# The first product of ten of the dense layer's sixteen weight groups by Strassen's scheme: seven products of sums of quarters in place of eight

## The chip, the cores and the metric

The kernel runs on one core of a Trainium2 chip. The metric is device time in microseconds for one execution, the median over runs. The core has five engines with a queue of instructions each: TensorE (PE in the profile, with PEld for its loads of weights), VectorE (DVE), ScalarE (ACT), GpSimd (POOL) and SyncE (SP), which issues most DMAs here.

## What is computed

Attention over a window of 32 keys and sums of 32-key blocks, then a dense layer of four experts, each weighted by its probability for each token, then a layer with eight experts of which each token takes one at most. The change is in the dense layer. Its reference, with N = 1536 tokens, D = 512, four experts and F = 1024 features:

```python
def _moe_ref(x, domain_probs, w1, w2):
    p = domain_probs / (domain_probs.sum(-1, keepdims=True) + 1e-09)
    out = np.zeros((N, D), dtype=np.float32)
    for e in range(E):
        h = np.maximum(x @ w1[e], 0.0)
        out += p[:, e:e + 1] * (h @ w2[e])
    return out
```

## The kernel before

Features are taken in 16 groups of 256, four to an expert. A group has two pieces of 128 features (`cc`), and x is cut into four chunks of 128 rows (`c`). Products are made in parts, so as to come near to float32: of each operand there is a high part (rounded, names with `h`) and a low part (the rest, names with `l`), and each product is three matmuls, high by high, low by high and high by low, into one bank of PSUM.

- **First product** (`part_a`, L357): for a block of 512 tokens and a piece of 128 features, 4 chunks x 3 matmuls of 512 columns into bank 0 or 1. The weights stand in the array, the tokens stream. ScalarE takes the relu out of the bank (L364, `hh`), VectorE the low part (L365, `hl`).
- **Second product** (`part_b`, L377): for each tile of 128 tokens 3 matmuls a piece, 6 a group, into banks 2 to 5. VectorE multiplies by the probability and adds to the result `acc` (L387).
- **Weights**: `load_w` issues two DMAs a group on SP into `raw`, 512 KB each; `split_w` rounds a half of them on ScalarE (L96) and subtracts on VectorE (L97). The parts of two groups stand side by side (`g % 2`), the raw weights of one.

Groups 0 and 1 run together with the attention, in blocks of two tiles (256 columns). Groups 2 to 13 go by themselves, three blocks of 512 tokens each; groups 14 and 15 run together, with the routing of the last layer between their blocks. The order of work up to group 13 is a scheduler's, which takes the program in the order of emission and moves instructions within each engine by its own costs; from group 14 on (`manual_schedule`) it is the order of emission. Each engine does its queue in order. The loop over `chunks` emits the first product of a piece and the second product of the piece before, and then a split of the next group's weights. `route_setup` (tables and memsets on GpSimd, two loads on SP) and 12 stores of zeros to `out` are emitted when the attention has ended.

Of the kernel before, what the change touches and what calls it, by code (L numbers as in the profile page):

```python
# [9 lines left out]
F32 = mybir.dt.float32  # L10
# [14 lines left out]
def attention_moe_kernel(  # L25
# [46 lines left out]
    wtiles = {}  # L72

    def load_w(g):
        wh = wps[g % 2].tile([P, 2 * KC * GF], F32R, name=f"wh{g}", tag="wh")
        wl = wps[g % 2].tile([P, 2 * KC * GF], F32R, name=f"wl{g}", tag="wl")
# [13 lines left out]
        wtiles[g] = (raw, wh, wl)  # L90

    def split_w(g, i):
        raw, wh, wl = wtiles[g]
        w = KC * GF // 2
        s, r = slice(i * w, (i + 1) * w), raw[i // 2][:, i % 2 * w : (i % 2 + 1) * w]
# [41 lines left out]
    # a band: the columns from 20 - 4 * i on average the rows of the i-th 128 tokens over 32  # L137
# [72 lines left out]
    def k_win(b, t):  # L210
        """Keys that the queries of a unit see, their sums behind them."""
# [15 lines left out]
    def fold_rows(dst, t):  # L227
        """Sums the eight rows of each partition on GpSimd."""
# [9 lines left out]
    def v_acc(b, i):  # L238
        """Sums over groups of tokens on TensorE."""
# [96 lines left out]
    chunks = []  # L336

    def moe_block(gs, t0, nt):
        """Work of a block of tokens with the weights of groups gs, one chunk of 128 features at a time."""
# [7 lines left out]
        def part_a(ci, c):  # L347
            g, cc = gs[ci // ncc], ci % ncc
            _, wh, wl = wtiles[g]
# [21 lines left out]
        def part_b(ci, t):  # L371
            g, cc = gs[ci // ncc], ci % ncc
            _, wh, wl = wtiles[g]
            hh, hl = hs[ci]
            f0 = KC * GF + cc * DM
# [26 lines left out]
    # parts of the base slots: (place of the expert in the order, its first rank)  # L402
# [11 lines left out]
    # slots: halves of the first product in parts, whether the second product is, engines of the low parts  # L414
# [4 lines left out]
    # slots whose parts are made from a slot on  # L419
# [52 lines left out]
    def route_block(t0, k):  # L472
        """Work that routes k tiles of tokens, in order; None where the next piece waits for VectorE."""
# [132 lines left out]
    def decode(name, c):  # L606
        """Rows and gates from sums of codes; a place that no token has gives a row behind the last."""
# [9 lines left out]
    def count_all(col):  # L617
        """Number of tokens listed so far for each expert, the same in each partition."""
# [4 lines left out]
    def early_pick():  # L623
        """Orders the experts by their tokens so far; the last two get more room."""
# [9 lines left out]
        # place in the lists of each place of the base slots  # L634
# [24 lines left out]
    def early_close():  # L659
        """Later tokens of the picked expert come behind the places of the early slot."""  # L660
# [9 lines left out]
    def list_sel(name, off, nt, done=None):  # L670
        """Marks, for 128 consecutive places of the lists, the tokens of the first nt tiles that stand there."""
# [76 lines left out]
    def load_units(limit=None):  # L748
        """Loads in order into the tiles that no emitted or coming reader needs."""
# [16 lines left out]
    def more_units(a, b):  # L766
        """Pairs of tiles of rows that have gone out."""
# [17 lines left out]
    def split_next():  # L785
        """High and low parts of the next half unit, into the place of one that the products have left."""
# [13 lines left out]
    def want_split(es, one, two, low):  # L800
        """Parts wanted by a slot: of the last halves of the first product, of the second; low: engines of the low parts."""
# [19 lines left out]
    def slot_trans(name, xg, b):  # L821
        """Rows of a slot the other way round: as they are, and in parts."""
# [4 lines left out]
        if one < 2:  # L827
            # the early slot's stand where rows have gone out
# [112 lines left out]
    # TensorE's clock rises only after some time of work  # L941
# [24 lines left out]
    def a_list():  # L966
        """Attention work in order of emission: (TensorE cost, function, unit completed)."""
# [108 lines left out]
    for g in range(2, last - 1):  # L1076
        for i in range(3):
            moe_block((g,), 4 * i, 4)
# [9 lines left out]
    rstack = ExitStack()  # L1088
# [12 lines left out]
    def expert(s):  # L1101
        """Register with the expert at place s of the order of the slots."""
# [20 lines left out]
    for ch in chunks:  # L1123
# [13 lines left out]
        if ch["gs"] == (last - 1,) and first and ch["t0"] == 0:  # L1137
            ctx.enter_context(tc.manual_schedule())
        micros = list(ch["a"])
# [18 lines left out]
        if p1:  # L1158
            if ch["last"] and blk == len(PH1) - 1:
                run_to(len(alist))  # L1160
                astack.close()
                rpool = rstack.enter_context(tc.tile_pool(name="route", bufs=1, side="right", reuse_waits="tile"))
# [8 lines left out]
                load_w(2)  # L1171
                for i in range(4):
                    split_w(2, i)
        elif not fin:
# [146 lines left out]
```

## Time and profile before

| | us |
|---|---|
| runs (three) | 714.49, 716.11, 717.57 |
| median | 716.11 |
| span of the profiled execution | 717.6 |
| TensorE busy | 696.9 |
| VectorE busy | 358.9 |
| ScalarE busy | 199.2 |
| GpSimd busy | 68.1 |

The span runs from the first to the last instruction of one execution. [...] Idle time is put down to the engine and the tile that was waited for. GpSimd's work lies in the attention and in the last layer; in the middle of the span it has none. Durations of single instructions hold for an engine alone; where operations of one kind follow each other their ends overlap a little with the next start, and a row of n gives the better price.

### The profile page before, as it was taken

To read this page: it belongs to the slowest core of one execution; us is meant where nothing else is said; L and a number is where in the kernel's file an instruction comes from. 1 tells how busy PE (TensorE), PEld (TensorE's weight loads), DVE (VectorE), ACT (ScalarE), POOL (GpSimd) and SP (SyncE) were. 2 spreads that over 40 slices of the span, in tenths; PEclk is the share of its full clock that TensorE was granted. 3 is DMA by queue.
4 is the path that set the end of the run, shared out by engine and by line. 5 is a ranking of instruction groups with operands and counts; after the bars stand their busy time and mean duration, and the time that the engine had idled before them with its cause. 6 is when DMAs were issued, how large, how long until landed. Compare 5 with 4: busy or idle time off the path is not lost. (4 is left out here: it accounts for less than half of the span.)

```text
span 717.6 us, 10481 instructions
## 1 busy us (share of the span) xinstructions
PE 696.9 (97%) x3951; PEld 553.9 (77%) x3951; DVE 358.9 (50%) x919; ACT 199.2 (28%) x505; POOL 68.1 (9%) x142
## 2 busy tenths in 40 slices
PE   6889999999999999999999999999999999799996
PEld 6779888888888888888888888888888888574361
DVE  5788655354353444353443544452525565585441
ACT  4556564221120212021221202021211223171340
POOL 5216400000000000000000000000000003331230
PEclk9999999999999999999999999999999999899999
DMA  9987211520101101010101101010100187467991
GB/s 233 234 208 168 63 46 24 207 87 0 59 14 46 59 0 59 1 58 1 59 0 59 37 22 59 0 59 1 58 1 0 60 311 268 142 247 281 412 409 53
DMA packets 39876, 73.77 MB, mean 103 GB/s; under 512 B 16740, under 2 KB 19812, under 8 KB 39824
## 3 DMA queue, kind: packets, MB, share of 16 engines
q1 hardware_dynamic: 38592, 70.31, 30.3%
q0 software_dynamic: 960, 2.25, 0.9%
q8 instruction: 32, 0.52, 0.3%
q10 hardware_dynamic: 272, 0.52, 0.2%
q14 instruction: 20, 0.16, 0.1%
HBM read 66.10 MB, written 7.86 MB: 103 GB/s over the span
## 5 line engine op out<-in xcount | busy, mean ns | idle before, releaser
L387 DVE SCALAR_TENSOR_TENSOR acc<-bank,pr,acc 128x512 f32<-128x512 f32 x163 | 113.3, 744 | 112.3 <-PE bank L377 112.3
L357 PE MATMUL bank<-xh,wh 128*128 128x512 f32 (+2 forms) x448 | 161.8, 363 | 0.0
L357 PE MATMUL bank<-xl,wh 128*128 128x512 f32 (+2 forms) x448 | 161.1, 360 | 0.0
L357 PE MATMUL bank<-xh,wl 128*128 128x512 f32 (+2 forms) x448 | 160.7, 359 | 0.0
L364 ACT ACTIVATE hh<-bank 128x512 fp32r<-128x512 f32 (+2 forms) x112 | 60.0, 536 | 345.6 <-PE bank L357 345.6
L377 PE MATMUL bank<-wh,hh 128*128 128x512 f32 x384 | 152.2, 396 | 0.0
L377 PE MATMUL bank<-wh,hl 128*128 128x512 f32 x384 | 146.8, 393 | 3.9 <-DVE hl L365 3.9
L377 PE MATMUL bank<-wl,hh 128*128 128x512 f32 x384 | 150.1, 391 | 0.0
L365 DVE SCALAR_TENSOR_TENSOR hl<-bank,hh 128x512 fp32r<-128x512 f32 (+2 forms) x112 | 68.3, 610 | 144.9 <-ACT hh L364 144.9
L357 PEld LDWEIGHTS bank<-xh,wh 128*128 128x128 f32 x448 | 84.1, 188 | 13.4 <-issue 0.4
L357 PEld LDWEIGHTS bank<-xl,wh 128*128 128x128 f32 x448 | 84.4, 188 | 12.8 <-DVE xl L333 0.2
L357 PEld LDWEIGHTS bank<-xh,wl 128*128 128x128 f32 x448 | 84.4, 188 | 11.9
L377 PEld LDWEIGHTS bank<-wh,hl 128*128 128x128 f32 x384 | 71.9, 188 | 19.6 <-DVE hl L365 4.8
L377 PEld LDWEIGHTS bank<-wh,hh 128*128 128x128 f32 x384 | 72.4, 188 | 16.2 <-issue 2.3
L377 PEld LDWEIGHTS bank<-wl,hh 128*128 128x128 f32 x384 | 72.4, 189 | 13.6 <-issue 0.2
L810 POOL DMA_INDIRECT xg<-out_dram,ixx x1 | 1.2, 1236 | 474.5 <-DVE acc L387 474.5
L289 ACT ACTIVATE sm<-sm,mn 128x120 f32<-128x120 f32 x96 | 36.7, 385 | 19.0 <-DVE mn L284 18.8
L96 ACT CAST wh<-raw 128x512 fp32r<-128x512 f32 x57 | 31.3, 618 | 30.4 <-PE bank L377 27.2
L97 DVE TENSOR_TENSOR wl<-raw,wh 128x512 fp32r<-128x512 f32 x60 | 37.7, 685 | 3.3 <-ACT wh L96 3.3
L273 PE MATMUL bank<-kw,qbd 128*128 128x120 f32 x192 | 27.3, 292 | 4.1 <-DMA qbd<-in_q_dram 3.7
L273 PEld LDWEIGHTS bank<-kw,qbd 128*128 128x128 f32 x192 | 24.7, 203 | 5.3 <-ACT kw L223 3.9
L284 DVE CUSTOM_DVE_ANT_0 sm<-bank,masks 128x120 f32<-128x120 f32 x96 | 21.3, 276 | 9.7 <-PE bank L273 9.6
(236 smaller groups left out, 629.7 us busy)
## 6 DMA issues: line engine op xcount, KB each, us to landing
raw<-in_moe_w_dram SPq DMA_DIRECT2D x30, 512.0 KB, 3.9
ra<-in_moe_w_dram SPq DMA_DIRECT2D x27, 512.0 KB, 9.1
rb<-in_moe_w_dram SPq DMA_DIRECT2D x21, 512.0 KB, 6.9
acc<-in_moe_w_dram SPq DMA_DIRECT2D x15, 512.0 KB, 9.3
vwin<-in_v_dram SPq DMA_DIRECT2D x24, 192.0 KB, 4.6
kt<-in_k_dram SPq DMA_DIRECT2D x8, 384.0 KB, 6.0
qbd<-in_q_dram SPq DMA_DIRECT2D x24, 128.0 KB, 5.6
out_dram<-xg SPq DMA_DIRECT2D x12, 256.0 KB, 2.9
```

Of the source, the lines that this page charges most:

```text
L96: (nc.gpsimd.tensor_copy if (g, i) in WPOOL else nc.scalar.copy)(wh[:, s], r)
L97: nc.vector.tensor_sub(wl[:, s], r, wh[:, s].bitcast(F32))
L273: nc.tensor.matmul(ps[:, h * WC : (h + 1) * WC], qb[b, t // 2][:, t % 2, h, :], kwin[b, t // 4][:, t % 4, h, :], start=True, stop=True,)
L284: nc.vector.tensor_tensor_reduce(out=sm[:, h, :], in0=ps[:, h * WC : (h + 1) * WC], in1=masks[:, m, :], scale=-0.125, scalar=3.0e38, op0=A ...
L289: nc.scalar.activation(sm[:, h, :], sm[:, h, :], AF.Exp, bias=mn[:, h : h + 1], scale=-1.0, accum_out=su[:, h : h + 1],)
L357: nc.tensor.matmul(b[:, :n], wt[:, f0 : f0 + P], xt[:, c, :], start=(c == 0 and i == 0), stop=(c == KC - 1 and i == 2),)
L364: nc.scalar.activation(hh[:, :n], b[:, :n], AF.Relu)
L365: nc.vector.scalar_tensor_tensor(out=hl[:, :n], in0=b[:, :n], scalar=0.0, in1=hh[:, :n].bitcast(F32), op0=ALU.max, op1=ALU.subtract,)
L377: nc.tensor.matmul(bank[2 + t], ht[:, t * P : (t + 1) * P], wt[:, f0 : f0 + DM], start=(ci == 0 and i == 0), stop=(ci == nch - 1 and i == 2),)
L387: nc.vector.scalar_tensor_tensor(out=a, in0=bank[2 + t], scalar=sc, in1=a, op0=ALU.mult, op1=ALU.add,)
L810: nc.gpsimd.indirect_dma_start(out=xg, out_offset=None, in_=out[:rows, :], in_offset=bass.IndirectOffsetOnAxis(ap=ix, axis=0), bounds_chec ...
```

## The change

For groups 4 to 13 (`SGROUPS`) the first product is no longer made block by block. The tokens are taken as two pairs of equal parts: `l`, tokens 512 to 1023 and 1024 to 1535 (512 columns a matmul), and `s`, tokens 0 to 255 and 256 to 511 (256 columns). x for a pair is cut into four quarters, two halves of the rows (256 each) by the two parts of the tokens, and the group's weights into four quarters, the two halves of the rows by the two pieces of features. In place of the eight products of quarters there are seven, of quarters and sums of quarters, each of 2 chunks x 3 matmuls (`burst`): p1, p5, p6, p3, p7, p2, p4 in that order. The sums between products are made in three ways: by summing on in a bank (p6 and p7 into the bank that holds a copy of p1; p3 into p5's; p2 into p1's; p4 into the bank of p1 + p6 + p7), by copies to SBUF on ScalarE (`s5`, `u2`) and by adds on VectorE (`u2` = p3's bank + `u2`; `s5` = p7's bank + `s5`).

- **Sums of x** (`x_sums`), once for all ten groups: 36 operations of 512 columns on VectorE (12 of them make x from its parts, 12 are sums, 12 low parts) and 12 roundings on ScalarE. They are emitted with groups 2 and 3, three steps after each chunk.
- **Sums of weights** (`w_steps`), each group: four operations on GpSimd, one of which overwrites a quarter of the raw weights, then rounded on ScalarE and subtracted on VectorE in two pieces.
- **Order** (`middle`): written out by hand from group 4 on. After each of the 14 products of a group stands one tile of the second product (six matmuls, the two pieces one behind the other), save after the third and the sixth product of the short pair; the steps for the next group's weights are dealt out by the table `at`. Tiles left over go on with the next group, the last seven with group 14. Tiles use banks 2 to 4 in turn.
- **Set-up of the routing**, its loads and the 12 stores of zeros: at the first piece of group 14. `load_w(15)` is ahead of them on SP. What the parts of weights are kept in is divided (`w_parts`), so that those of the second product are taken later.
- One matmul into bank 7 is added ahead of group 4.

```diff
+    SGROUPS = range(4, E1 * NG - 2)
+    PAIRS = {"l": (4 * P, 4 * P), "s": (0, 2 * P)}
...
+            def whole(i, j):
+                h, l = x_quarter(p, i, j, c)
+                nc.vector.tensor_add(xt[f"{i + 1}{j + 1}"], h.bitcast(F32), l.bitcast(F32))
+            def total(i, a, b):
+                nc.vector.tensor_sub(ts[i], a, b)
+                nc.scalar.copy(xsum[p][0][:, i, c, :], ts[i])
+            def low(i):
+                nc.vector.tensor_sub(xsum[p][1][:, i, c, :], ts[i], xsum[p][0][:, i, c, :].bitcast(F32))
...
+    def w_steps(g):
...
+            t = scr["w"].tile([P, 3, 2, P], F32, name=f"ws{g}", tag="ws")
+            tt = nc.gpsimd.tensor_tensor
+            tt(out=t[:, 1], in0=a11, in1=a21, op=ALU.subtract)
+            tt(out=a21, in0=a21, in1=a22, op=ALU.add)
+            tt(out=t[:, 0], in0=a21, in1=a11, op=ALU.subtract)
+            tt(out=t[:, 2], in0=a12, in1=t[:, 0], op=ALU.subtract)
...
+        def sum_parts(i):
+            (h, l), t = wtiles[g][3:]
+            s = slice(0, 2) if i == 0 else slice(2, 3)
+            nc.scalar.copy(h[:, s], t[:, s])
+            nc.vector.tensor_sub(l[:, s], t[:, s], h[:, s].bitcast(F32))
...
+            lambda: load_w(g), sums if mid else no, lambda: split_w(g, 1), lambda: split_w(g, 0),
+            (lambda: sum_parts(0)) if mid else no, (lambda: sum_parts(1)) if mid else no,
+            lambda: split_w(g, 2), lambda: split_w(g, 3),
...
+        ba, be, bb = bank[state_["i"] % 2], bank[6], bank[7 - 2 * (state_["i"] % 2)]
...
+        def burst(b, w, x, start):
+            for c in range(2):
+                for i, (a, m) in enumerate(((0, 0), (0, 1), (1, 0))):
+                    nc.tensor.matmul(
+                        b[:, :n], w[c][a], x[c][m], start=start and c == 0 and i == 0, stop=c == 1 and i == 2,
...
+        def p1():
+            burst(ba, wq(0, 0), xq(0, 0), True)
+            nc.scalar.copy(bb[:, :n], ba[:, :n])
+        def p5():
+            burst(be, wq(1, 0), xs(0), True)
+            nc.scalar.copy(tmp("s5"), be[:, :n])
+        def p6():
+            burst(bb, wsum(0), xs(1), False)
+            nc.scalar.copy(tmp("u2"), bb[:, :n])
+        def p3():
+            burst(be, wsum(2), xq(1, 1), False)
+            nc.vector.tensor_add(fs["u2"], be[:, :n], fs["u2"])
+            part(0, 1, fs["u2"])
+        def p7():
+            burst(bb, wsum(1), xs(2), False)
+            nc.vector.tensor_add(fs["s5"], bb[:, :n], fs["s5"])
+            part(1, 1, fs["s5"])
+        def p2():
+            burst(ba, wq(0, 1), xq(1, 0), False)
+            part(0, 0, ba[:, :n])
+        def p4():
+            burst(bb, wq(1, 1), xs(3), False)
+            part(1, 0, bb[:, :n])
...
+        nc.tensor.matmul(bank[7], wh[:, :P], wh[:, :512], start=True, stop=True)
+        at = {0: (0,), 2: (1,), 4: (2,), 5: (3,), 7: (4,), 8: (5,), 9: (6,), 11: (7,)}
+        for g in SGROUPS:
+            nxt = w_steps(g + 1)
+            i = 0
+            for p in "ls":
+                bursts, tiles = pair_work(g, p, state_)
+                for b in bursts:
+                    b()
+                    for k_ in at.get(i, ()):
+                        nxt[k_]()
+                    if i not in (9, 12) and todo:
+                        todo.pop(0)()
+                    i += 1
+                todo += tiles
```

`part` takes the relu (ScalarE) and its low part (VectorE) as before, from a bank or from `u2` and `s5`.

Three places show what the engines' queues hold now. In the names, `hl5_4_1` is the low part of the relu of group 5, block of tiles from 4 on, piece 1; `hls01_s5_01` the same of group 5's short pair; `w2l6` is the low part of group 6's second weights, `wsl6` that of its sums; `u2s5` and `s5s5` are the short pair's sums of group 5.

VectorE in the middle, group 5, before: splits, then low parts and updates of the result.

```order
L97 TENSOR_TENSOR wl6_2445<-raw6_0_2446,wh6_2444 128x512 x2
L97 TENSOR_TENSOR wl6_2445<-raw6_1_2447,wh6_2444 128x512 x2
L365 SCALAR_TENSOR_TENSOR hl5_0_1_2463<-bank1_62,hh5_0_1_2462 128x512
L365 SCALAR_TENSOR_TENSOR hl5_4_0_2493<-bank0_61,hh5_4_0_2492 128x512
L387 SCALAR_TENSOR_TENSOR acc_74<-bank2_63,pr_75,acc_74 128x512
L387 SCALAR_TENSOR_TENSOR acc_74<-bank3_64,pr_75,acc_74 128x512
L387 SCALAR_TENSOR_TENSOR acc_74<-bank4_65,pr_75,acc_74 128x512
L387 SCALAR_TENSOR_TENSOR acc_74<-bank5_66,pr_75,acc_74 128x512
L365 SCALAR_TENSOR_TENSOR hl5_4_1_2527<-bank1_62,hh5_4_1_2526 128x512
```

VectorE in the middle now, short pair of group 5, from the last sum of weights on:

```order
L474 TENSOR_TENSOR wsl6_2497<-ws6_2491,wsh6_2496 128x256
L570 SCALAR_TENSOR_TENSOR acc_74<-bank3_64,pr_75,acc_74 128x512
L102 TENSOR_TENSOR w2l6_2621<-raw6_1_2458,w2h6_2620 128x512
L544 TENSOR_TENSOR u2s5_2618<-bank6_67,u2s5_2618 128x256
L525 SCALAR_TENSOR_TENSOR hls01_s5_01_2632<-u2s5_2618,hhs01_s5_01_2631 128x256
L570 SCALAR_TENSOR_TENSOR acc_74<-bank4_65,pr_75,acc_74 128x512
L549 TENSOR_TENSOR s5s5_2601<-bank5_66,s5s5_2601 128x256
L525 SCALAR_TENSOR_TENSOR hls11_s5_11_2650<-s5s5_2601,hhs11_s5_11_2649 128x256
```

Between the updates of `acc` there are now adds out of banks 6 and 5, and the split of the next group's second weights stands right ahead of them.

VectorE at the end of groups 0 and 1, before (block of tiles from 10 on, then group 2):

```order
L365 SCALAR_TENSOR_TENSOR hl0_10_0_1656<-bank0_61,hh0_10_0_1655 128x256
L365 SCALAR_TENSOR_TENSOR hl0_10_1_1680<-bank1_62,hh0_10_1_1679 128x256
L365 SCALAR_TENSOR_TENSOR hl1_10_0_1702<-bank0_61,hh1_10_0_1701 128x256
L97 TENSOR_TENSOR wl2_1825<-raw2_0_1826,wh2_1824 128x512 x2
L97 TENSOR_TENSOR wl2_1825<-raw2_1_1827,wh2_1824 128x512 x2
L365 SCALAR_TENSOR_TENSOR hl1_10_1_1724<-bank1_62,hh1_10_1_1723 128x256
L365 SCALAR_TENSOR_TENSOR hl2_0_0_1851<-bank0_61,hh2_0_0_1850 128x512
```

The same place now, from the fourth operation behind `hl0_10_0` on; three more of the same kinds stand ahead of these rows:

```order
L431 TENSOR_TENSOR t1l0_1801<-x22l0_1799,t0l0_1800 128x512
L428 TENSOR_TENSOR x11l1_1950<-xh1_79,xl1_80 128x512
L102 TENSOR_TENSOR w1l2_1751<-raw2_0_1752,w1h2_1750 128x512
L370 SCALAR_TENSOR_TENSOR hl0_10_1_1684<-bank1_62,hh0_10_1_1683 128x256
L428 TENSOR_TENSOR x12l1_1951<-xh1_79,xl1_80 128x512
L435 TENSOR_TENSOR xsll_1744<-t0l0_1800,xslh_1743 128x512
L435 TENSOR_TENSOR xsll_1744<-t2l0_1802,xslh_1743 128x512
L431 TENSOR_TENSOR t3l0_1803<-x21l0_1798,t1l0_1801 128x512
L428 TENSOR_TENSOR x22l1_1953<-xh1_79,xl1_80 128x512
L435 TENSOR_TENSOR xsll_1744<-t1l0_1801,xslh_1743 128x512
L370 SCALAR_TENSOR_TENSOR hl1_10_0_1706<-bank0_61,hh1_10_0_1705 128x256
```

Sums of x (L428 makes x from its parts, L431 a sum, L435 a low part) and the first splits of group 2 stand between the low parts of the relus.

GpSimd behind the attention's last copies, before:

```order
L266 COPY vwin2_168<-vsm1_912 24x512
L266 COPY vwin3_169<-vsm1_912 24x512
L430 IOTA io_1739 128x128
L433 IOTA cf_1742 128x12
L434 IOTA cf_1742 128x12
L438 MEMSET tri_1747 128x128
```

GpSimd in the middle now (40 rows of this kind, four for each of groups 4 to 13, stand between those copies and the tables):

```order
L463 TENSOR_TENSOR ws6_2491<-raw6_0_2457 128x256
L464 TENSOR_TENSOR raw6_0_2457<-raw6_0_2457 128x2x128
L465 TENSOR_TENSOR ws6_2491<-raw6_0_2457 128x256
L466 TENSOR_TENSOR ws6_2491<-raw6_0_2457,ws6_2491 128x256
L463 TENSOR_TENSOR ws7_2732<-raw7_0_2698 128x256
```

The tables (`io`, `cf` and on) have moved behind them, to group 14.

## Rows read from the trace of the kernel before

**Rows 1.** The page's first part: busy time, share of the span, instructions

```profile
PE 696.9 (97%) x3951; PEld 553.9 (77%) x3951; DVE 358.9 (50%) x919; ACT 199.2 (28%) x505; POOL 68.1 (9%) x142
```

**Rows 2.** Busy times by stretch; one group of weights in the middle

```profile
core 0: us, PE busy (x) PEld busy (x) DVE busy (x) ACT busy (x) POOL busy (x), PEclk, DMA share, GB/s
182.60:215.30 32.70, 32.70 (x146) 27.08 (x145) 14.36 (x22) 5.78 (x10) 0.00 (x0) 1.00 0.11 34
```

**Rows 3.** The waits: who for whom, us in total, times, longest

```profile
ACT hh L364 <- PE bank L357: 345.6, 95, 4.8
```

**Rows 4.** Timeline of ScalarE: start, duration, line, operation, idle time before it

```profile
153.79 0.60 ACT L364 ACTIVATE hh<-bank 128x512 fp32r<-128x512 f32 x1 [4.84 <-PE bank L357]
159.23 0.60 ACT L364 ACTIVATE hh<-bank 128x512 fp32r<-128x512 f32 x1 [4.84 <-PE bank L357]
```

**Rows 5.** Timeline, all engines: a product's last matmul and its reader

```profile
300.25 0.39 PE L357 MATMUL bank<-xh,wl 128*128 128x512 f32 x1
300.67 0.60 ACT L364 ACTIVATE hh<-bank 128x512 fp32r<-128x512 f32 x1 [4.84 <-PE bank L357]
```

**Rows 6.** Timeline of TensorE: matmuls of 256 columns back to back

```profile
131.93 0.28 PE L357 MATMUL bank<-xh,wh 128*128 128x256 f32 x1
...
134.33 0.40 PE L377 MATMUL bank<-wh,hh 128*128 128x512 f32 x1
```

**Rows 7.** Groups by line and shape: weight loads (busy, mean ns)

```profile
L357 PEld LDWEIGHTS bank<-xh,wl 128*128 128x128 f32 x448 | 84.4, 188 | 11.9
```

**Rows 8.** The same view: operations on VectorE, ScalarE and GpSimd

```profile
L387 DVE SCALAR_TENSOR_TENSOR acc<-bank,pr,acc 128x512 f32<-128x512 f32 x163 | 113.3, 744 | 112.3 <-PE bank L377 112.3
L365 DVE SCALAR_TENSOR_TENSOR hl<-bank,hh 128x256 fp32r<-128x256 f32 x28 | 11.7, 416 | 17.4 <-ACT hh L364 17.3
L364 ACT ACTIVATE hh<-bank 128x256 fp32r<-128x256 f32 x28 | 10.6, 379 | 17.5 <-PE bank L357 17.4
L97 DVE TENSOR_TENSOR wl<-raw,wh 128x512 fp32r<-128x512 f32 x60 | 37.7, 685 | 3.3 <-ACT wh L96 3.3
L96 ACT CAST wh<-raw 128x512 fp32r<-128x512 f32 x57 | 31.3, 618 | 30.4 <-PE bank L377 27.2 <-DMA raw<-in_moe_w_dram 3.1
L230 POOL TENSOR_TENSOR acc<-acc 96x256 f32<-96x256 f32 x4 | 3.4, 842 | 0.0
L798 POOL TENSOR_TENSOR sl<-ra,sh 128x512 fp32r<-128x512 f32 x7 | 8.9, 1283 | 14.5 <-ACT sh L797 14.5
```

**Rows 9.** Timeline, end of the first two groups: VectorE, then TensorE

```profile
133.68 0.42 DVE L365 SCALAR_TENSOR_TENSOR hl<-bank,hh 128x256 fp32r<-128x256 f32 x1 [0.79 <-ACT hh L364]
139.38 2.50 DVE L97 TENSOR_TENSOR wl<-raw,wh 128x512 fp32r<-128x512 f32 x4 [1.20 <-ACT wh L96]
140.90 0.62 PE L377 MATMUL bank<-wh,hl 128*128 128x512 f32 x2
```

**Rows 10.** Timeline: VectorE and GpSimd at the same time, two places

```profile
71.39 0.74 POOL L230 TENSOR_TENSOR acc<-acc 96x256 f32<-96x256 f32 x1
71.48 0.42 DVE L365 SCALAR_TENSOR_TENSOR hl<-bank,hh 128x256 fp32r<-128x256 f32 x1
669.22 3.43 DVE L798 TENSOR_TENSOR sl<-acc,sh 128x512 fp32r<-128x512 f32 x1
669.57 1.29 POOL L798 TENSOR_TENSOR sl<-acc,sh 128x512 fp32r<-128x512 f32 x1
670.83 1.26 POOL L798 TENSOR_TENSOR sl<-ra,sh 128x512 fp32r<-128x512 f32 x1
```

**Rows 11.** Set-up of the routing: issues, a relu; loads (count, KB, us to landing)

```profile
125.20 7.26 SPq L1168 DMA_DIRECT2D out_dram<-xg  x12
534.59 0.60 ACT L364 ACTIVATE hh<-bank 128x512 fp32r<-128x512 f32 x1 [4.84 <-PE bank L357]
559.69 0.40 SPq L486 DMA_DIRECT2D out_dram<-acc  x1
raw<-in_moe_w_dram SPq DMA_DIRECT2D x30, 512.0 KB, 3.9
```

More of the change, by code (lines that the diff above doesn't have):

```diff
@@ L72, in attention_moe_kernel, with w_parts @@
     wtiles = {}
+    def w_parts(g, i):
+        return [wps[g % 2].tile([P, KC * GF], F32R, name=f"w{i}{n}{g}", tag=f"w{i}{n}") for n in "hl"]
     def load_w(g):
-        wh = wps[g % 2].tile([P, 2 * KC * GF], F32R, name=f"wh{g}", tag="wh")
-        wl = wps[g % 2].tile([P, 2 * KC * GF], F32R, name=f"wl{g}", tag="wl")
+        w1t = w_parts(g, 1)
         if g == 0:
@@ L348, in part_a @@
             g, cc = gs[ci // ncc], ci % ncc
-            _, wh, wl = wtiles[g]
+            wh, wl = wtiles[g][1]
             if c == 0:
@@ new lines, in middle @@
+    def middle(todo):
+        todo = list(todo)
+        state_ = dict(i=0, b=0)
+        wh = wtiles[SGROUPS[0]][1][0]
+        nc.tensor.matmul(bank[7], wh[:, :P], wh[:, :512], start=True, stop=True)
[13 more added lines that the diff above has]
+                todo += tiles
+        return todo
@@ L1075, in attention_moe_kernel @@
         moe_block(gs, t0, n)
-    for g in range(2, last - 1):
+    for g in range(2, SGROUPS[0]):
         for i in range(3):
@@ L1138, in attention_moe_kernel @@
             ctx.enter_context(tc.manual_schedule())
+            prev = dict(gs=(last - 2,), last=True, b=middle(prev["b"]))
+            load_w(last)
         micros = list(ch["a"])
@@ L1161, in attention_moe_kernel @@
                 astack.close()
+                scr["w"] = sstack.enter_context(tc.tile_pool(name="msum", bufs=1, side="right", reuse_waits="tile"))
+                for p_, (_, n_) in PAIRS.items():
+                    xsum[p_] = [scr["w"].tile([P, 4, 2, n_], F32R, name=f"xs{p_}{q_}") for q_ in "hl"]
+                xsteps = x_sums(tstack.enter_context(tc.tile_pool(name="mtmp", bufs=1, side="right", reuse_waits="tile")))
+                load_w(2)
+                for i in range(4):
+                    split_w(2, i)
+        elif not fin:
+            if g < SGROUPS[0] - 1:
+                if first and ch["t0"] == 0:
+                    load_w(g + 1)
+                    pend = 0
+                elif pend < 4:
+                    split_w(g + 1, pend)
+                    pend += 1
+            else:
+                if first and ch["t0"] == 0:
+                    wsteps = w_steps(g + 1)
+                for _ in range(1 + (len(wsteps) < 5)):
+                    if wsteps:
+                        wsteps.pop(0)()
+            for _ in range(3):
+                xsteps.pop(0)()
+            if not xsteps:
+                tstack.close()
+                scr["h"] = sstack.enter_context(tc.tile_pool(name="mh", bufs=1, side="right", reuse_waits="tile"))
+        if ch["gs"] == (last - 1,) and ch["t0"] == 0 and ch["ci"] == 0:
+            if True:
+                sstack.close()
                 rpool = rstack.enter_context(tc.tile_pool(name="route", bufs=1, side="right", reuse_waits="tile"))
@@ L1170, in attention_moe_kernel @@
                 free += [rap.tile([P, FF], F32, name=f"ra{i}") for i in range(NRA)]
[L1171 to L1174, printed above, removed]
-            if first and ch["t0"] == 0:
-                load_w(g + 1)
-                pend = 0
-            elif pend < 4:
-                split_w(g + 1, pend)
-                pend += 1
-            elif g == last - 2:
-                load_w(last)
         if ch["gs"] == (last,) and ch["t0"] == 0 and ch["last"]:
```

96 lines of the change are left out of this document (90 added, 6 removed).

## The prediction

> **What bounds the kernel now.** I read the page's busy times first, then the busy times by stretch, then the waits, then the timeline. TensorE is busy for 696.9 of 717.6 us [rows 1]. In the dense layer's middle, one stretch of 32.7 us (one group of weights) shows TensorE busy throughout at a granted clock of 1.00, VectorE for 14.36 us, ScalarE for 5.78 us, GpSimd for nothing [rows 2]. The waits say the same from the other side: ScalarE waits 95 times for TensorE's first product, 345.6 us in all [rows 3]. So in the groups that are changed each TensorE instruction that goes away is time, provided that the sums which take its place stay inside the idle time of the other engines.
>
> **What is taken from TensorE.** The relu of the first product comes every 159.23 - 153.79 = 5.44 us [rows 4]; between two of them lie 24 matmuls of 512 columns, so one costs 5.44 / 24 = 0.2267 us. From 131.93 to 134.33 lie 20 matmuls of 256 columns, back to back, each with a weight load of its own: 2.40 / 20 = 0.120 us each [rows 6]. Before, the first product of a group is 3 blocks x 24 matmuls of 512 columns: 72 x 0.2267 = 16.32 us. After, the long pair (two quarters of 512 tokens) needs 7 products x 6 matmuls of 512 columns, 42 x 0.2267 = 9.52 us, and the short pair 42 matmuls of 256 columns, 42 x 0.120 = 5.04 us: 14.56 us. The second product keeps its 72 matmuls. So 16.32 - 14.56 = 1.76 us a group, **17.6 us for ten**. One matmul is added ahead of the ten groups: 0.2 us.
>
> **What is added elsewhere, a group.** VectorE keeps 12 updates of the result (12 x 0.744 = 8.9 us) and gets two adds and four low parts for either pair (6 x 0.685 for the long one, at the price of a two-input operation of 512 columns, and 6 x 0.416 for the short: 6.6 us) and six low parts of weights and weight sums (five at 0.685, one of half the width near 0.42: 3.8 us): 19.3 us of about 31 [rows 8]. ScalarE gets seven operations a pair (7 x 0.60 and 7 x 0.38) and six casts at 0.62 or less: about 10 us [rows 5, 8]. Neither can bound the group by its sum; what can hurt is a chain. The chain with the least room is in the short pair: its last product, p4, sums on in the bank that holds p1 + p6 + p7, and may only start when VectorE has taken that sum out (the add to s5). On VectorE this add stands behind four others.
>
> I work it out from the end of p6's matmuls as zero. TensorE then does p3 in 0.72 (6 x 0.120), a tile of the second product in 1.36 (6 x 0.2267), p7 in 0.72, a tile in 1.36 and p2 in 0.72 us, so p4 is due at 4.88. A reader of a bank starts about 0.2 us after the matmuls' slot: 300.67 after 300.25 + 0.23 [rows 5]. ScalarE: the copy to u2 ends at 0.58, the cast of weights behind it at 1.14. VectorE: low part of those weights 1.15 to 1.84; add to u2 1.77 to 2.19; relu on ScalarE to 2.60; low part to 3.05; update of the result to 3.71; the awaited add to 4.05. **Room: about 0.8 us**, if nothing holds VectorE up. Behind the last product stands all that TensorE has left, so a slip beyond that counts in full.
>
> GpSimd does. It gets four two-input operations of 128x256 a group for sums of weights; where they run is set by when VectorE has read the sums before (about -0.6 on this scale; the load for them is issued five products earlier and lands in 3.9 us [rows 11]). A two-input operation of 96x256 takes 0.842 us in the mean and 0.74 at best [rows 8, 10], so the run ends between 2.4 and 2.8. The trace shows what that does: a VectorE subtraction with both operands in SBUF that met two GpSimd operations took 3.43 us instead of 0.69, until both were done, while one that reads a bank of PSUM kept its 0.42 us beside GpSimd [rows 10]. The low part of the weights has both operands in SBUF, so it ends near 3.0 (with 0.74) or 3.4 (with 0.842), and the last product slips by 0.4 or 0.8 us. [...] I take 0.37 us, by the 0.74 that is nearest in shape, in the eight groups during which such a run falls (the first two sets of sums are made earlier): **3.0 us, between 0 and 6.2** (it can't be below nothing, since TensorE has no pause there to lose).
>
> **Lead-in.** The sums of x are 36 VectorE operations of 512 columns, 0.62 us each in a row (2.50 / 4) [rows 9]: 22 us, which the scheduler puts between the last block of the first two groups and the end of the third. Between the low parts of blocks (0, 10) and (1, 10) it puts twelve of them and splits in place of one wait: the first ends near 134.5 instead of 134.1 [rows 9], then 12 x 0.62 + 0.34 + 0.42 brings the second to 142.7. TensorE wants it at 140.90 [rows 9], so it waits about 1.8 us. By the same count the next three low parts are there 0.3 to 1 us before TensorE comes to them, unless the first GpSimd run (3.0 to 3.4 us) meets this full VectorE; I take 1.2 us for that. **3.0 us, between 0 and 5.** The first changed group has few tiles of the second product to put between its products (four of three matmuls): its long chain is late by the same count by about **0.5 us, between 0 and 1.5**.
>
> **Moved.** The set-up of the routing (memsets and tables on GpSimd, two small loads and the 12 stores of zeros, 7.3 us of issue on SP [rows 11]) goes from the end of the attention to the next to last group. GpSimd and SP are empty there; the tiles of the second product that free its memory end about 12 us into that group, the set-up and the stores take about 12 more, and the first store that waits for them comes 28 us into the group before (the relu of its first block at 534.59 closes 2.7 us of products, so it begins near 531.7; the store is at 559.69) and some 7 us later now, since seven tiles are left over [rows 11]. I cost it at nothing, covered by about 10 us; loads of weights stand ahead of it on SP, none behind it that is due there.
>
> **Sum.** -17.6 + 0.2 + 3.0 + 3.0 + 0.5 = -10.9 us. The profiled execution has a span of 717.6, with nothing to speak of around it: it is like the longest of the three runs (717.57), and 1.5 above their median. 717.6 - 10.9 = 706.7, which is **705** on the median's scale.
>
> **Rivals.**
> - All waits are covered: GpSimd and VectorE take turns so that the low part slips by less than 0.8 us, and the sums of x fit. -17.4 us, 699. For it: 20 us in 31 is little for VectorE. Against: the twelve operations counted above.
> - All waits at their upper ends: -17.6 + 0.2 + 6.2 + 5 + 1.5 = -4.7, 711, and with runs of GpSimd a little longer up to 714.
> - **Slower than before:** the GpSimd run is the bound. If its operations cost what 128x512 cost there (1.283 us [rows 8]: two pieces of 128 each are another pattern than any in the trace), a run is 5.1 us and ends at 4.5, the add at 7.3, the last product is 2.4 us late, and the groups that have it gain nothing. With the same wait at the other low part on the way (both operands in SBUF too) it is 3 us or more: 8 x 3 + 3.7 - 17.6 = +10, 726. It decides from about 1.7 us of wait a group. Against it: 0.74 and 0.842 for 256 columns.
> - Short matmuls don't pay: each costs its weight load of 0.188 us [rows 7], so the short pair takes 42 x 0.188 = 7.9 us instead of 5.4 before: ten times +2.5, less 13.6 for the long pair, +11 and the waits, 729. The rows of 131.93 speak against it.
> - The change does nothing for the time, since another engine bounds the group: needs over 31 us of VectorE; there are 19.3.
>
> **Chances.** Forecast (701.5 to 709) 0.56; all covered (698 to 701.5) 0.18; upper ends 0.14, more than half of it below 712.5; GpSimd as the bound 0.08; short matmuls 0.02; nothing 0.02. A measurement of this kernel tells about 0.5% from no change, 3.6 us. Faster by more: 0.56 + 0.18 + 0.08 = 0.82; within: 0.06 + 0.02 = 0.08; slower: 0.10. Eight in ten lie from 699 to 711.
>
> **What would show it.** In the profile after: matmuls of the short pair 0.120 us apart; a period of a changed group of 30.9 (nothing waits) to 31.3 us; in the waits TensorE for VectorE's add of the partial sum, 0.4 us about eight times; VectorE low parts of weights of 2 us instead of 0.69 beside GpSimd operations of 0.74; 1 to 3 us of TensorE waiting for a low part between 139 and 160 us; no wait for the stores of zeros. Wrong would be: GpSimd operations of over 1.1 us, a period above 32, or TensorE waits at the start of every product.

## The result, and the profile after

The changed kernel takes 710.79 us (median of 20 runs, 707.44 to 713.52), the kernel before in the same comparison 716.40: a ratio of 0.990, 95% interval 0.9885 to 0.9919, so 7.0 us faster (5.8 to 8.2); the two medians by themselves lie 5.6 us apart. I had forecast 705, 10.9 us faster, in a range of 699 to 711. Sign and range hold, the range by 0.2 us only; by the ratio a third of the gain that I forecast is missing, by the medians half.

The page's first line after answers to [rows 1]:

```profile
PE 686.7 (97%) x4072; PEld 547.7 (78%) x4072; DVE 425.5 (60%) x1035; ACT 245.5 (35%) x617; POOL 103.5 (15%) x182
```

TensorE is busy for 686.7 us instead of 696.9, VectorE for 425.5 instead of 358.9, and the span of this execution is 705.7. The two profiled executions are not a fair pair: this one lies 3 us below its kernel's median, the one before 3 us above. So I compare stretches. The relus on ScalarE mark TensorE's progress: the first block behind the attention, the last block of group 3, and the last block of 512 tokens of group 14. Timeline of ScalarE, before:

```profile
133.27 0.39 ACT L364 ACTIVATE hh<-bank 128x256 fp32r<-128x256 f32 x1 [2.82 <-PE bank L357]
...
144.27 0.60 ACT L364 ACTIVATE hh<-bank 128x512 fp32r<-128x512 f32 x1 [3.08 <-PE bank L357]
...
202.75 0.60 ACT L364 ACTIVATE hh<-bank 128x512 fp32r<-128x512 f32 x1 [4.84 <-PE bank L357]
...
551.13 0.60 ACT L364 ACTIVATE hh<-bank 128x512 fp32r<-128x512 f32 x1 [4.84 <-PE bank L357]
```

And after:

```profile
130.71 0.39 ACT L369 ACTIVATE hh<-bank 128x256 fp32r<-128x256 f32 x1 [2.82 <-PE bank L362]
...
143.39 0.60 ACT L369 ACTIVATE hh<-bank 128x512 fp32r<-128x512 f32 x1 [2.37 <-PE bank L362]
...
202.69 0.60 ACT L369 ACTIVATE hh<-bank 128x512 fp32r<-128x512 f32 x1 [4.84 <-PE bank L362]
...
540.13 0.60 ACT L369 ACTIVATE hh<-bank 128x512 fp32r<-128x512 f32 x1 [4.84 <-PE bank L362]
```

From the first mark to the last it is 417.86 us before and 409.42 after: 8.4 us gained. To the second mark (the lead-in) 11.00 and 12.68: 1.7 lost. To the third (groups 2 and 3) 58.48 and 59.30: 0.8 lost, of which 0.23 is the added matmul. To the fourth 348.38 and 337.44: 10.9 gained where I had counted 17.6. **So 6.7 us are missing in the changed groups themselves.** Their period is read off ScalarE's copy behind the first product, which comes once a group:

```profile
263.27 0.57 ACT L532 COPY bank<-bank 128x512 f32<-128x512 f32 x1 [2.34 <-PE bank L509]
...
294.78 0.57 ACT L532 COPY bank<-bank 128x512 f32<-128x512 f32 x1 [2.34 <-PE bank L509]
```

31.51 us, in each of eight periods, where I had counted 30.9 and named 31.3 as the most. The busy times of one of them answer to [rows 2]; the columns are the window, its length, and busy time and instructions of PE, PEld, DVE, ACT and POOL, then the granted clock, DMA share and GB/s:

```profile
263.27:294.78 31.51, 31.51 (x157) 26.39 (x156) 18.85 (x30) 9.70 (x21) 3.28 (x4) 1.00 0.10 34
```

TensorE is busy from end to end at a granted clock of 1.00, VectorE for 18.85 us (I had counted 19.3). TensorE waits for nothing here. The waits of its weight loads between 120 and 560 us say so too; the columns are who waits for whom, us in total, times, longest:

```profile
PEld bank L382 <- DVE hl L370: 2.3, 3, 1.3
...
PEld bank L509 <- DVE s5l L549: 0.5, 1, 0.5
```

The first is the lead-in, the second one wait of 0.5 us in the first changed group. What is left is the distance of the matmuls. Timeline of TensorE, one tile of the second product (six matmuls of 512 columns) and the first matmul behind it:

```profile
297.38 0.39 PE L568 MATMUL bank<-w2h,hhl_l 128*128 128x512 f32 x1
297.61 0.40 PE L568 MATMUL bank<-w2l,hhl_l 128*128 128x512 f32 x1
...
298.77 0.39 PE L509 MATMUL bank<-xslh,wsh 128*128 128x512 f32 x1
```

Each is shown for 0.39 or 0.40 us, and the next starts 0.23 or 0.24 us after it: the distance between the starts is what one costs. (298.77 - 297.38) / 6 = 0.232 us, where [rows 4] gave 0.2267, in an unbroken row, with the same operation and shape. Over all changed groups the mean is 0.2327. A group has 114 matmuls of 512 columns, so 114 x 0.006 = 0.7 us; the 42 of 256 columns are a little nearer than the 0.120 that I took (0.1185) and give 0.06 back. That is the 0.6 us a group, 5.6 us in the nine groups behind the first.

### The profile page after: what moved, and what is told of

The parts are those of the page before. It is cut to its first block, busy times and chain, and to the rows that moved or that the text cites. A ratio compares the mean times of both kernels' runs of the same rounds, so it can differ in the third digit from the quotient of the medians.

```text
span 705.7 us, 10995 instructions
## 1 busy us (share of the span) xinstructions
PE 686.7 (97%) x4072; PEld 547.7 (78%) x4072; DVE 425.5 (60%) x1035; ACT 245.5 (35%) x617; POOL 103.5 (15%) x182
## 5 line engine op out<-in xcount | busy, mean ns | idle before, releaser
L362 PE MATMUL bank<-xh,w1h 128*128 128x256 f32 (+2 forms) x208 | 68.6, 334 | 0.0
L362 PE MATMUL bank<-xl,w1h 128*128 128x256 f32 (+2 forms) x208 | 67.7, 326 | 0.0
L362 PE MATMUL bank<-xh,w1l 128*128 128x256 f32 (+2 forms) x208 | 67.4, 324 | 0.0
L382 PE MATMUL bank<-w2h,hh 128*128 128x512 f32 x144 | 58.7, 408 | 0.0
L382 PE MATMUL bank<-w2h,hl 128*128 128x512 f32 x144 | 54.6, 403 | 4.3 <-DVE hl L370 4.3
L382 PE MATMUL bank<-w2l,hh 128*128 128x512 f32 x144 | 56.8, 394 | 0.0
L362 PEld LDWEIGHTS bank<-xh,w1h 128*128 128x128 f32 x208 | 39.1, 189 | 4.3 <-DVE hl L370 0.4
L362 PEld LDWEIGHTS bank<-xl,w1h 128*128 128x128 f32 x208 | 39.4, 189 | 3.3
L362 PEld LDWEIGHTS bank<-xh,w1l 128*128 128x128 f32 x208 | 39.3, 189 | 2.6
L568 PE MATMUL bank<-w2h,hhl_l 128*128 128x512 f32 x80 | 31.8, 397 | 0.0
```

What stands on the lines that cost most here:

```text
L362: nc.tensor.matmul(b[:, :n], wt[:, f0 : f0 + P], xt[:, c, :], start=(c == 0 and i == 0), stop=(c == KC - 1 and i == 2),)
L382: nc.tensor.matmul(bank[2 + t], ht[:, t * P : (t + 1) * P], wt[:, f0 : f0 + DM], start=(ci == 0 and i == 0), stop=(ci == nch - 1 and i == 2),)
L568: nc.tensor.matmul(b, a, w[:, s], start=i == 0 and k_ == 0, stop=i == 1 and k_ == 2)
```

## The experiments

What is new for TensorE in the changed groups: runs of six matmuls instead of twelve, the steps between 256 and 512 columns, and operands in new places of SBUF. In the kernel before all operands of the dense layer (x, relu parts, weights) begin at addresses with the remainder 64 modulo 256 bytes. The tiles that the change added (sums of x, weight sums, most of the relu parts) stand at the other end of SBUF and begin at the remainder 224. The remainders are read off the built programs.

| run | operands moved | remainder of those moved, of the rest | distance, 512 columns | median us | ratio to before (95%) |
|---|---|---|---|---|---|
| before | none | 64 | 0.2267 | 716.4 | 1 |
| after | new ones | 224, 64 | 0.2327 | 710.8 | 0.990 (0.9885 to 0.9919) |
| e1 | as after | 224, 64 | 0.2327 | 708.3 | 0.9865 (0.983 to 0.990) |
| e2 | as after | 192, 64 | 0.231 | 708.1 | 0.986 (0.982 to 0.9895) |
| e5 | as after | 64, 64 | 0.228 | 703.1 | 0.983 (0.979 to 0.987) |
| e8 | as e5, sums of x held back | 64, 64 | 0.228 | 700.2 | 0.978 (0.974 to 0.982) |
| e10 | as e8, no GpSimd | 64, 64 | 0.228 | 702.4 | 0.979 (0.972 to 0.985) |
| e3 | before, all | 96 | 0.2267 | 717.7 | 1.000 (0.998 to 1.003) |
| e4 | before, relu parts; weights and x of tokens 0 to 511 | 96; 128; other x 64 | 0.2325 | 726.2, one run | |
| e6 | before, relu parts by 128 bytes | 192, 64 | 0.231 | 726.2, one run | |
| e9 | before, relu parts by 256 bytes | 64, 64 | 0.2267 | 719.3, one run | |
| e7 | before, relu parts by 512 bytes | 64, 64 | 0.2267 | 714.3, one run | |

The distance is the mean over the matmuls of 512 columns in the changed groups (for before and its relatives from 160 to 520 us), gaps by waits left out. Each ratio is to the kernel before in the same comparison, where its median was between 716.4 and 718.1 us; a kernel with one run has no ratio, and its distance and its group, read off its trace, carry the argument.

**e1, the changed kernel again.**

> The changed kernel once more, unedited, for the spread between executions and a second profile. In the first profile after, matmuls of 512 columns in the changed groups stand 0.233 us apart instead of 0.2267 at a granted clock of 1.00, so a group takes 31.5 us instead of 30.9. If that belongs to the program (every theory below), the period of groups 5 to 13 is 31.5 us again; if it was an accident of one execution, 30.9. The profile before was 3 us longer than its median and the profile after 3 us shorter than its own: this one should come out near 709 us, with the difference to the first in the attention, by dips of the granted clock, not in the changed groups.

The period is 31.51 again:

```profile
264.79 0.57 ACT L532 COPY bank<-bank 128x512 f32<-128x512 f32 x1 [2.34 <-PE bank L509]
...
296.30 0.57 ACT L532 COPY bank<-bank 128x512 f32<-128x512 f32 x1 [2.34 <-PE bank L509]
```

It belongs to the program. Theories A, B and C, which the expectation of e2 spells out, are still open.

**e2, new operands at multiples of 64 bytes.**

```diff
+                pad = sstack.enter_context(tc.tile_pool(name="pad", bufs=1, side="right", reuse_waits="tile"))
+                pad.tile([P, 8], F32, name="pad")
                 scr["w"] = sstack.enter_context(tc.tile_pool(name="msum", bufs=1, side="right", reuse_waits="tile"))
```

> The changed kernel with 32 unused bytes a partition put at the end of SBUF, so that the sums of x, the weight sums and the parts of the relu that the change added begin at multiples of 64 bytes as all operands of TensorE in the kernel before do; in the changed kernel they begin at 32 over a multiple. Nothing else is changed. Theory A (an operand that begins at 32 over a multiple of 64 costs TensorE some 6 ns a matmul): spacing of 512-column matmuls back near 0.2267 to 0.229 us, a period of 30.9 to 31.1 us, 4 to 6 us less in all than the changed kernel. Theory B (the step from matmuls of 256 to 512 columns does it, each time anew): period stays 31.5 us, time as the changed kernel. Theory C (runs of six matmuls with waits between them keep TensorE's sequencer from running ahead): the same, 31.5 us.

```profile
263.52 0.57 ACT L532 COPY bank<-bank 128x512 f32<-128x512 f32 x1 [2.30 <-PE bank L509]
...
294.89 0.57 ACT L532 COPY bank<-bank 128x512 f32<-128x512 f32 x1 [2.30 <-PE bank L509]
```

31.37 us: 0.14 of the 0.6. Theory A as I put it falls, and with it most of the 4 to 6 us that it promised. B and C are not decided by it; what C says of TensorE's sequencer was an assumption of mine that no run shows.

**e3 and e4, the kernel before with operands moved: all of them by 32 bytes; the relu's parts by 32 bytes and, without intent, the weights by 64.**

```diff
+    pad = mstack.enter_context(tc.tile_pool(name="pad", bufs=1))
+    pad.tile([P, 8], F32, name="pad")
     mp = mstack.enter_context(tc.tile_pool(name="moe1", bufs=1))
```

In e4 the first pad stands ahead of `hbuf` instead, and a second one of the same size behind it. The two together move what stands behind them by 64 bytes. So e4 is not what its expectation says: in the built program the relu's parts begin at the remainder 96, the weights and x of tokens 0 to 511 at 128, and only x of the other tokens stays at 64.

> The kernel before with 32 unused bytes a partition ahead of x, the relu's parts and the weights, so that all operands of the dense layer begin at 32 over a multiple of 64. No other edit. Theory A: 512-column matmuls in groups 2 to 13 go from 0.2267 to about 0.233 us, a group from 32.65 to 33.5 us, the whole 10 us slower than before or more. Theories B and C: no change, 716 us.

> The kernel before with only the relu's two parts (what is loaded into the array in the second product) shifted by 32 bytes; x and the weights stay at multiples of 64. Theory A, if what is loaded counts: the second product's matmuls at about 0.233 us; if only what streams counts: 0.2267 as before. Theories B and C: 0.2267 throughout.

Relus on ScalarE, six blocks (144 matmuls, one group) apart, of e3 and then of e4:

```profile
185.28 0.60 ACT L366 ACTIVATE hh<-bank 128x512 fp32r<-128x512 f32 x1 [4.84 <-PE bank L359]
...
217.92 0.60 ACT L366 ACTIVATE hh<-bank 128x512 fp32r<-128x512 f32 x1 [4.84 <-PE bank L359]
```

```profile
184.78 0.60 ACT L368 ACTIVATE hh<-bank 128x512 fp32r<-128x512 f32 x1 [5.00 <-PE bank L361]
...
201.58 0.60 ACT L368 ACTIVATE hh<-bank 128x512 fp32r<-128x512 f32 x1 [5.00 <-PE bank L361]
207.13 0.60 ACT L368 ACTIVATE hh<-bank 128x512 fp32r<-128x512 f32 x1 [4.95 <-PE bank L361]
212.65 0.60 ACT L368 ACTIVATE hh<-bank 128x512 fp32r<-128x512 f32 x1 [0.54 <-PE bank L361]
218.25 0.60 ACT L368 ACTIVATE hh<-bank 128x512 fp32r<-128x512 f32 x1 [5.00 <-PE bank L361]
```

32.64 us for e3, as before; 33.47 for e4. The blocks inside e4's group tell more than was planned. Those that end at 207.13 and 212.65 hold the first products of tokens 0 to 511, with x and weights both at 128; they take 5.55 and 5.52 us, the blocks around them 5.60. Matmul by matmul, from 160 to 520 us, these first products stand 0.228 us apart, those of the other tokens (x at 64, weights at 128) 0.233, and the second product (relu's parts at 96, weights at 128) 0.233. This is the experiment that showed the way: with all operands at 96 a group takes the 32.64 us that it took at 64 (theory A falls for good), yet a kernel that has neither Strassen's scheme, nor 256 columns in these groups, nor runs of six gets matmuls as slow as the changed one's, 0.2325 us for 0.2327, when its operands have **different** remainders. B and C can't explain that.

**e5, e6 and e7: the same remainder modulo 512 for the new operands, and moves of 128 and 512 bytes in the kernel before.** e5 is e2 with a pad of 40 elements (160 bytes) instead of 8; e6, e7 and e9 below are e4 with other sizes; in them the two pads add up to 512 or 1024 bytes, so the weights and x keep the remainder 64 and the relu's parts alone can change theirs. The 32 bytes that these expectations ascribe to the relu's parts alone are e4's, to be read as said above; e6 is the clean case.

> The changed kernel with 160 unused bytes a partition at the end of SBUF, so that all new operands of TensorE (sums of x, weight sums, relu parts) begin at the same remainder modulo 512 bytes as the old ones (320). Moving all operands of the kernel before by 32 bytes cost nothing, moving only the relu's parts cost 8 us or more (0.2325 us a matmul instead of 0.2267), and multiples of 64 with other remainders modulo 512 brought the changed kernel's group only from 31.51 to 31.37 us. Theory D: what TensorE loads and what it streams must begin at the same remainder of some power of two of up to 512 bytes; then 512-column matmuls lock at 0.2267 us again, the period is 30.9 to 31.0 us and the whole is 5 us below the changed kernel. Theory B (the steps from 256 to 512 columns) leaves the period at 31.3 us or more.

> The kernel before with only the relu's two parts moved by 128 bytes against x and the weights. Theory D: if the power of two is 256 or 512, the second product (and with it the rest) goes to about 0.232 us a matmul of 512 columns and the whole to 724 us or so; if it is 64 or 128, nothing changes. Theory A (only 32 over a multiple of 64 hurts) and theory B: nothing changes.

> The kernel before with only the relu's two parts moved by 512 bytes against x and the weights: the control of the run with 128. Theory D: 0.2267 us a matmul of 512 columns as before, 716 us, if the power of two is 512 or less; slower spacing again if it is 1024 or more. Theory B: 0.2267.

ScalarE's copies in e5, and the relus of one group in e6 and in e7:

```profile
260.71 0.57 ACT L532 COPY bank<-bank 128x512 f32<-128x512 f32 x1 [2.30 <-PE bank L509]
...
291.69 0.57 ACT L532 COPY bank<-bank 128x512 f32<-128x512 f32 x1 [2.30 <-PE bank L509]
```

```profile
187.12 0.60 ACT L368 ACTIVATE hh<-bank 128x512 fp32r<-128x512 f32 x1 [5.00 <-PE bank L361]
...
220.39 0.60 ACT L368 ACTIVATE hh<-bank 128x512 fp32r<-128x512 f32 x1 [5.00 <-PE bank L361]
```

```profile
187.77 0.60 ACT L368 ACTIVATE hh<-bank 128x512 fp32r<-128x512 f32 x1 [4.84 <-PE bank L361]
...
220.41 0.60 ACT L368 ACTIVATE hh<-bank 128x512 fp32r<-128x512 f32 x1 [4.84 <-PE bank L361]
```

e5: 30.98 us, 0.53 less in each group, which makes 5 us in ten, and by the runs 0.983 where the changed kernel has 0.9865 and 0.990, 3 to 5 us. e6: 33.27 us for 32.64; e7: 32.64. Theory D holds in these runs, and theory C falls, as e5 keeps its runs of six. The loss does not stay with the matmuls whose operands differ: in e6 those of the first product, all at 64, stand 0.229 us apart, those of the second 0.233; in the changed kernel, where products and tiles of six alternate, matmuls with equal remainders take 0.232 us and the others 0.233. Theory B keeps a small part: the 0.1 us that e5 still has above the counted 30.88 stands behind the short products. Timeline of TensorE in e5, the first matmul of a tile and the first behind it, after a product of 256 columns:

```profile
247.92 0.40 PE L568 MATMUL bank<-w2h,hh_l 128*128 128x512 f32 x1
...
249.31 0.28 PE L509 MATMUL bank<-xssh,w1h 128*128 128x256 f32 x1
```

and after one of 512:

```profile
229.53 0.39 PE L568 MATMUL bank<-w2h,hhl_l 128*128 128x512 f32 x1
...
230.89 0.39 PE L509 MATMUL bank<-xslh,w1h 128*128 128x512 f32 x1
```

1.39 and 1.36 us, and five tiles of the first kind in a group.

**e9, 256 bytes.**

> The kernel before with only the relu's two parts moved by 256 bytes against x and the weights. 32 and 128 bytes made the matmuls of 512 columns slower (0.2325 and 0.231 us), 512 did not (0.2267). If the power of two of theory D is 512: near 0.230 us, 722 us or more; if it is 256: 0.2267 and about 715 us.

```profile
186.31 0.60 ACT L368 ACTIVATE hh<-bank 128x512 fp32r<-128x512 f32 x1 [4.84 <-PE bank L361]
...
218.95 0.60 ACT L368 ACTIVATE hh<-bank 128x512 fp32r<-128x512 f32 x1 [4.84 <-PE bank L361]
```

32.64 us with 256 bytes, where 128 gave 33.27: by these two runs the power of two is 256. (Its one run of 719.3 lies within what the kernel before does.)

**e8, the sums of x held back**, on top of e5:

```diff
                 hs[ci] = (hh, hl)
+                scr["hl"] = hl
...
             def whole(i, j):
                 h, l = x_quarter(p, i, j, c)
+                nc.vector.tensor_copy(xt[f"{i + 1}{j + 1}"][:, 0, :1], scr["hl"][:, :1].bitcast(F32))
                 nc.vector.tensor_add(xt[f"{i + 1}{j + 1}"], h.bitcast(F32), l.bitcast(F32))
```

> The run with 160 bytes, and besides each operation that makes x from its parts gets a small copy (one column, from the low part of the latest relu) ahead of it into the same tile, so that the scheduler can't put the sums of x ahead of group 2's first relu: they are spread over groups 2 and 3. My prediction put 3.0 us (0 to 5) on the lead-in; the profiles after show TensorE losing 1.7 us to it by the first block of group 2 and 0.6 us more by 160 us. If VectorE's queue there is the cause, both are gone (2.3 us below the run with 160 bytes, less what twelve copies cost where VectorE bounds); if it is the first groups' own work (weights, splits), nothing changes.

First, the wait in the changed kernel. VectorE's low part at the end of the first two groups stands behind six operations of 0.6 us without a pause (those from 135.73 on), and TensorE waits for it (the brackets name the idle time and who ended it):

```profile
135.40 0.42 DVE L370 SCALAR_TENSOR_TENSOR hl<-bank,hh 128x256 fp32r<-128x256 f32 x1
...
138.74 0.69 DVE L435 TENSOR_TENSOR xsll<-t1l,xslh 128x512 fp32r<-128x512 f32 x1
139.34 0.42 DVE L370 SCALAR_TENSOR_TENSOR hl<-bank,hh 128x256 fp32r<-128x256 f32 x1
```

```profile
138.56 0.40 PE L382 MATMUL bank<-w2l,hh 128*128 128x512 f32 x1
139.81 0.73 PE L382 MATMUL bank<-w2h,hl 128*128 128x512 f32 x2 [0.85 <-DVE hl L370]
```

In e8 VectorE has pauses there again, and ScalarE's marks stand 11.01 us apart (11.00 before, 12.68 after):

```profile
130.81 0.38 ACT L369 ACTIVATE hh<-bank 128x256 fp32r<-128x256 f32 x1 [2.82 <-PE bank L362]
...
141.82 0.60 ACT L369 ACTIVATE hh<-bank 128x512 fp32r<-128x512 f32 x1 [2.80 <-PE bank L362]
```

No wait of TensorE for a low part is left in groups 0 to 3. e8 is at 0.978 where e5 was at 0.983: 3 us, but the two intervals overlap. The traces are sharper: from the first block behind the attention to the last block of group 3 it is 69.77 us in e8 and 72.00 in e5, so 2.2 us, as expected (2.3). **e8 is the fastest kernel of this study**: 700.2 us, 2.2% below before (1.8 to 2.6).

**e10, without the sums on GpSimd**, on top of e8: the four operations run for group 4 only.

> The gated run with 160 bytes, and the weight sums on GpSimd left out from group 5 on (the sums of group 4 are rounded and used again, so that part of the computation is left out): nothing runs on GpSimd in the changed groups. It prices the term of 3.0 us that my prediction gave to GpSimd and VectorE shutting each other out. By that term a group would take 0.37 us less than with the sums, 30.6 instead of 30.98 us, and the whole 3 us less. By the trace after (VectorE's subtraction waits for one GpSimd operation, 1.15 instead of 0.69 us, and the awaited add is still in time) nothing changes: 30.98 us, and 700 us as with the sums.

```profile
262.17 0.57 ACT L537 COPY bank<-bank 128x512 f32<-128x512 f32 x1 [2.30 <-PE bank L514]
...
293.15 0.57 ACT L537 COPY bank<-bank 128x512 f32<-128x512 f32 x1 [2.30 <-PE bank L514]
```

30.98 us as with the sums, and 0.979 for 0.978. GpSimd costs the end nothing.

## Why the prediction was right in sign and promised too much, step by step

- **The count of matmuls (-17.6).** The number of instructions was right, the price failed, and this is the step that made the forecast too good. I took 0.2267 us from [rows 4] and carried it over to all matmuls of 512 columns, though the change gives TensorE operands in new places. The runs of the kernel before show that price where all operands have one remainder modulo 256 bytes (0.2267 in before, e3, e7 and e9) and a higher one where they have not (0.2325 in e4, 0.231 in e6); the rows of before hold the first case alone. Measured: 0.2327 in the changed groups, which makes 5.6 us over nine groups and some 0.7 us more in the first changed group and the tiles behind the last. e5 gives 0.53 of the 0.6 us a group back by the pad alone. The price of 0.120 for 256 columns [rows 6] was right (0.1185).
- **GpSimd against VectorE (+3.0, between 0 and 6.2).** Wrong: it is nothing (e10: 30.98 us a group with the sums and without). VectorE's operation does get longer beside GpSimd's, but by less than I took. VectorE's low part of weights and the GpSimd operations around it, after:

```profile
255.78 1.16 DVE L102 TENSOR_TENSOR w2l<-raw,w2h 128x512 fp32r<-128x512 f32 x1 [0.88 <-ACT w2h L101]
...
258.76 0.41 DVE L549 TENSOR_TENSOR s5s<-bank,s5s 128x256 f32<-128x256 f32 x1
```

```profile
255.66 0.74 POOL L465 TENSOR_TENSOR ws<-raw 128x256 f32<-128x256 f32 x1
256.47 1.06 POOL L466 TENSOR_TENSOR ws<-raw,ws 128x256 f32<-128x256 f32 x1
```

  The low part takes 1.16 us instead of 0.69 beside two GpSimd operations, and the second of them takes 1.06 us where the first takes 0.74. The low part ends at 256.94, the run of GpSimd at 257.53. I had let it end behind that run, by [rows 10], where the operation of 3.43 us ended behind both. There the second GpSimd operation starts as the first ends (670.83 after 669.57 + 1.29); here 0.08 us lie between two. Whether that decides was not tried. The other half of the step was right: the awaited add ends at 258.76 + 0.41 = 259.17, and the last product's first matmul starts at 259.58, so of the 0.8 us of room 0.47 went and the rest covered the end:

```profile
259.46 0.28 PE L509 MATMUL bank<-xh,w1l 128*128 128x256 f32 x1
259.58 0.28 PE L509 MATMUL bank<-xssh,w1h 128*128 128x256 f32 x1
```

  So the rival "all waits are covered" was right on this wait, with a slip of 0.47 us where it named less than 0.8, and wrong on the time, since the price of a matmul was not among its terms.
- **Lead-in (+3.0, between 0 and 5).** Right in its cause: 1.7 us up to the first relu of group 2 (I had 1.8 for the place, in one wait; there are two, since the low part of block (0, 10) is late as well) and 0.6 in groups 2 and 3 (I had 1.2). e8 took it away and gained 2.2 us by the traces.
- **First changed group (+0.5) and the added matmul (+0.2).** Right: one wait of 0.5 us for the add to `s5` of the long pair, and 0.23.
- **The moved set-up (0).** Right: TensorE waits for none of it, and from the last block of group 14 to the end of the span nothing is lost (551.13 to 717.6 before, 540.13 to 705.7 after: 166.5 and 165.6 us).
- **The sum, and its scale.** By the stretches: -17.6 + 6.3 (distances) + 1.7 + 0.6 (lead-in) + 0.5 + 0.2 = -8.3, against 8.4 read off the marks and 7.0 (5.8 to 8.2) and 9.7 (7.4 to 12) in the two comparisons of runs. "Nothing to speak of around the span" was a slip as well: the profiled run after took 707.44 us with a span of 705.7, so 1.7 us lie around it, and the profiled execution before was 3 us above its median, not 1.5. Neither changes the 705, which is the median less the 10.9.
- **The range held by luck.** The price was 6.3 us off, and the waits that I charged and that did not come (GpSimd's 3.0 and 0.7 of the lead-in) hid 3.7 of it. 710.79 lies where I had put the rival with all waits at their upper ends, and none of the waits stood there.

No rival of mine had this cause. The one that put a higher price on matmuls (each short one costs its weight load) named the wrong ones: the short matmuls kept their price (0.1185 us for 0.120), and the long ones, which I took as known, did not (0.2327 for 0.2267).

## What to carry to other kernels

Here the price of a matmul went with the places of its operands: 0.2267 us for 512 columns in the kernel before, 0.2327 in the changed groups. So where a change gives an engine operands in new tiles, a price read from the trace of before is an estimate until the first trace after, and the range has to hold that. With 160 unused bytes a partition all that TensorE loads and streams began at the same remainder modulo 256 bytes, which was worth 0.53 us a changed group (e5): where TensorE bounds a kernel, such a pad deserves a run. Work that is "free" on an idle engine still wants a place in its queue: the same 36 operations cost 2.2 us or nothing (72.00 us in e5, 69.77 in e8, over the same blocks), by whether a scheduler may put them ahead of what TensorE waits for.

## What the hardware did that I had not expected

Here the weights of a matmul are loaded while the one ahead of it runs: in the timeline of the loads, those for the first two matmuls of the tile shown with the result, which start at 297.38 and 297.61, start with the matmul ahead of each, at 297.15 and 297.38, and take 0.19 us.

```profile
297.15 0.19 PEld L568 LDWEIGHTS bank<-w2h,hhl_l 128*128 128x128 f32 x1
297.38 0.19 PEld L568 LDWEIGHTS bank<-w2l,hhl_l 128*128 128x128 f32 x1
```

In the runs in which what is loaded and what streams begin at different remainders modulo 256 bytes, a matmul of 512 columns with a load of 128 took 231 to 233 ns in the mean (after, e2, e4, e6) instead of 226.7, at the same granted clock of 1.00 (before, after, e4 and e6). Differences of 32 and 64 bytes (e4), 128 (e6 and e2) and 160 (after) did it, 256 and 512 didn't (e9, e7), nor did moving all by 32 (e3). Other differences, other shapes and whether load or stream loses the time were not tried. In e6 no remainder but that of the loaded operand of the second product was changed, and the group went from 32.64 to 33.27 us.

Behind a step from 256 to 512 columns the matmuls of e5 stood 234, 236, 229, 232 and 231 ns apart in the mean before they came back to 227, as in the tile of e5 that took 1.39 us. In after, behind the first matmul after the waits of TensorE that end at 139.81, 154.63 and 158.57 us, it took eight, six and ten matmuls of 224 to 240 ns before 226 and 227 were back. With tiles of six behind short products that cost 0.1 us a group, once the remainders were equal. The kernel before shows the same behind the 256 columns of [rows 6], where the tile from 134.33 on took 1.39 us (233, 236, 228, 233, 231 and 226 ns); my sum priced such tiles at 1.36.
